# Attention and routed experts on one core: remainders of 64 rows as transposes, two PTb buffers, spread weight loads

## The chip, the cores and the metric

The kernel runs on one core of one Trainium2 chip. The metric is the time of one execution on the device in microseconds (us), the median of several runs. A second number comes from a profiled execution: its span, from the first to the last instruction. Engines: PE is TensorE's matmul queue, PEld its weight loads, DVE the vector engine, ACT the scalar engine, POOL is GpSimd, SP issues most DMAs.

## The reference

Eight batches of eight heads, 576 positions, head size 64. Attention keeps only the scores within `tau` of a row's maximum; its output becomes the input of a mixture of experts with one chosen expert of eight for each token.

```python
scores = scale * q @ k.T
thresh = max(scores, axis=-1) - tau
scores = where(scores >= thresh, scores, -1e9)
attn = exp(scores - max(scores)); attn = attn / (sum(attn) + 1e-9)
x = (attn @ v), heads side by side              # 4608 tokens x 512
e = argmax(x @ w_gate)                          # one expert of 8
y = relu(x @ w1[e]) @ w2[e]                     # 512 -> 1024 -> 512
out = softmax(x @ w_gate)[e] * sigmoid(x @ w_output_gate)[e] * y
```

## The kernel before, in words

There are two stages: attention (to about 480 us), then the experts. All engines but SP run in the order in which the program writes their instructions, so the order of the Python code is the order of each engine's queue.

A unit is one head of two batches, side by side as the two halves `a` = 0, 1 of 64 partitions. There are 32 units, two to an iteration `m`, and 16 iterations of `T` = 9 steps (`run`, L319). The step is `s`, the running number `g`. A step takes one block `t` of 128 query rows: steps 0 to 3 the blocks of the even unit, 5 to 8 those of the odd one, and step 4 the last 64 rows of both.

In step `g` the following is issued:

- `scores` (L129): PE computes scores into `ps` (two buffers of two banks for a step); DVE copies them out scaled, with the row minimum (L152); POOL makes the threshold `thr` (L159).
- In steps 1 and 5 `x_rows` (L283): PE turns the finished X of an earlier unit into rows and router logits, in the two single banks `pr` (pool `ps_r`) and `pa` (pool `ps_a`). ACT copies them out as `xl` (L345). The first write goes to `pr`.
- `exps` (L162): two exponentials on ACT, `p` from `s`, one for each half.
- V products by the table `AV` (`av_units`, L236): ten products of transposed probabilities with V for one unit, spread over steps 6, 7, 8, 0 (even unit) and 2, 3, 4 (odd). Four go into `pa`; a middle one takes the remainder rows for both banks and ends with the copy of X out of `pa` (L251); four go into `pb`, a tile of the bank `pr`, and end with the copy of X out of it (L258), in steps 0 and 4. The middle one is in steps 2 and 7, which are `CROSS`.
- The transposes of step `g - 2`: keys lie in 9 pieces of 128, of which the ninth holds the 64 remaining keys of both halves. `blocks` (L220) turns the first eight pieces by 16 transposes of 64 rows (L226) into `pt` (two banks, one buffer), which ACT copies to PTa or PTb (L231, L234). `remainder` (L199) turns the ninth.
- The masks of step `g - 1` on DVE (L179), which read `p`.
- `logits`, `inverse` (L267: an addition and a reciprocal on DVE, 128x10), hooks, and a step of the router (`rt.advance`).

`remainder` has two forms. In steps 1, 3, 5, 6 and 8 it is two transposes of 64 rows (L203), each into a corner of a bank that is open at that time or fresh, with one ACT copy each (L208). In steps 0, 2, 4 and 7 it is a pair of full products with the identity (L211; each is two instructions in the trace) into one bank, and one ACT copy (L216). In steps 2 and 7 they are issued ahead of the middle V product, into the bank that `pb` will use.

PTa holds the transposed probabilities of query rows 0 to 255, PTb those of the other 320, each in one buffer. The last 64 rows of the odd unit are produced before PTb is free for that unit, so they go to PTc, and a DMA on ACT's queue (L382) moves them to PTb in step 0.

Experts: a raw weight chunk is two loads of 512 KB (`load`, L793); four raw buffers. The hook at `end - 15` steps (L1238) calls `begin`, which issues four chunks, each after the latest `thr` (the gate). POOL scatters finished rows by indirect DMA (L531) in the meantime.

Of the kernel before, what the change touches and what calls it, by code (L numbers as in the profile page):

```python
# [20 lines left out]
class Attention:  # L21
# [6 lines left out]
    AV = {0: (-2, 2), 2: (-1, 4), 3: (-1, 2), 4: (-1, 2), 6: (0, 3), 7: (0, 1), 8: (0, 2)}  # L28
    CROSS = (2, 7)
    ROWS = {1: -2, 5: -1}  # L30
    LOGITS = {3: -2, 7: -1}
    INVERSE = ((7, 0), (2, 1))
# [70 lines left out]
    def warm_up(self, n):  # L103
        nc = self.nc
        wt = self.w2.tile([P, 512], BF16, name="wt")
        nc.vector.memset(wt, 0.0)
        self.wt = wt
        self.keep_warm(n)
# [79 lines left out]
    def turned(self, u, t):  # L188
        if t == 0:
            self.PTa = self.w2.tile([P, self.NK, self.QA], F32, name="PTa")  # L190
        if t == 2:
            self.PTb = self.w2.tile([P, self.NK, self.S - self.QA], F32, name="PTb")
        if t == self.NB:
            self.PTc = self.w2.tile([P, self.NK, 64], F32, name="PTc")
            return [self.PTb[:, :, self.QA :], self.PTc]
        q = self.PTa if t < 2 else self.PTb
        return [q[:, :, t % 2 * P : t % 2 * P + P]]

    def remainder(self, dst, p, pair=None, fresh=2, rest=None):  # L199
        nc, hs, M, RB = self.nc, self.half, self.M, self.NK - 1  # L200
        if pair:
            for h in range(2):
                nc.tensor.matmul(  # L203
                    pair[h], p[hs[h], M : M + P], self.ident[hs[h], hs[h]], start=h == fresh or fresh > 1, stop=True,
                    is_transpose=True, skip_group_check=True,
                )
            at = lambda h: dst[0][:, RB, 64 * h : 64 * h + 64] if len(dst) == 1 else dst[h][:, RB]
            return lambda h: nc.scalar.copy(at(h), pair[h])  # L208
        for pp in hs:
            o = M + pp.start  # L210
            nc.tensor.matmul(rest[pp, 0:P], p[:, o : o + 64], self.ident, start=True, stop=True, skip_group_check=True)  # L211

        def out():
            w = P // len(dst)
            for h, d in enumerate(dst):
                nc.scalar.copy(d[:, RB], rest[:, h * w : h * w + w])  # L216

        return out

    def blocks(self, dst, p, outs=()):  # L220
        nc, id_, hs, RB = self.nc, self.ident, self.half, self.NK - 1
        pt = self.ps_t.tile([P, 1024], F32, name="pt")
        for b in range(RB):
            for h in range(2):
                o, k0 = h * 512 + b * 64, (b + b // 4) * P
                nc.tensor.transpose(pt[:, o : o + 64], p[hs[h], k0 : k0 + P], id_[hs[h], hs[h]])  # L226
        for f in outs:
            f()
        if len(dst) == 1:
            d = dst[0][:, 0:RB].rearrange("p b (h j) -> p b h j", j=64)  # L230
            nc.scalar.copy(d, pt.rearrange("p (h b j) -> p b h j", h=2, j=64))  # L231
        else:
            for h, d in enumerate(dst):
                nc.scalar.copy(d[:, 0:RB], pt[:, h * 512 : h * 512 + 512].rearrange("p (b j) -> p b j", j=64))  # L234

    def av_units(self, u):  # L236
# [10 lines left out]
        pb, N = self.bank(), self.PTb.shape[2]  # L247
# [14 lines left out]
    def bank(self):  # L262
        if self.pb is None:
            self.pb = self.ps_r.tile([P, 512], F32, name="pr")
        return self.pb

    def inverse(self, m, i):  # L267
        if i == 0:
            self.rinv[m] = self.w3.tile([P, 2, 10], F32, name="rinv", bufs=2)
        r, s = self.rinv[m][:, i], self.sums[m][:, i]  # L270
        self.nc.vector.tensor_scalar(r, s, 1e-9, None, op0=ALU.add)
        self.nc.vector.reciprocal(r, r)
        if i:
            self.sums.pop(m)
# [44 lines left out]
    def run(self, hooks):  # L319
        nc, T, G, rt = self.nc, self.T, self.G, self.router  # L320
        W, NB = self.XW, self.NB
        st, pr, av, xls, later, held = {}, {}, {}, {}, None, None
        self.prep_first()
        for g in range(G + self.TAIL):
# [12 lines left out]
            if xu is not None:  # L337
# [3 lines left out]
                if turn:  # L341
                    out = self.remainder(dst, pr[g2], [x[:, 5 * W : 5 * W + 64] for x in ps])
                xl = xls[xu] = self.w2.tile([P, 2, 5, W], F32, name="xl")
                for a in (1, 0):
                    nc.scalar.copy(xl[:, a].rearrange("p j w -> p (j w)"), ps[a][:, 0 : 5 * W])  # L345
                    if turn:
                        out(a)
# [8 lines left out]
            if turn and xu is not None:  # L356
                self.blocks(dst, pr.pop(g2))
            soon = s in self.EARLY or g == G - 1
            if g < G and not soon:
                pr[g] = self.exps(u, t, *st[g])  # L360
            if s in self.AV:
                du, n = self.AV[s]
                au = 2 * m + du
                if 0 <= au < self.nu:
# [4 lines left out]
                    if s in self.CROSS:  # L369
                        if turn:  # L370
                            dst, o = [], self.S - self.QA
                            held = self.remainder(dst, pr[g2], rest=self.bank()[:, o : o + P])
                        next(av[au])
            if turn and xu is None:
                p = pr.pop(g2)
                u2, t2 = self.at(g2)
                if held is None:
                    dst = []
                dst.extend(self.turned(u2, t2))
                if u2 % 2 and t2 == 2:  # L380
                    if g < G:
                        nc.scalar.dma_start(self.PTb[:, :, self.QA :], self.PTc)  # L382
                pair = None
                if self.pa is not None:
                    rest = self.ps_r.tile([P, 512], F32, name="pr")
                    pair = [self.pa[:, self.S - self.QA : self.S - self.QA + 64], rest[:, 0:64]], 1
                elif self.pb is not None and held is None:
                    rest = self.ps_a.tile([P, 512], F32, name="pa")
                    pair = [rest[:, 0:64], self.pb[:, 448:512]], 0
                if pair:  # L390
                    out = self.remainder(dst, p, *pair)
                    outs = [lambda: out(0), lambda: out(1)]
                elif held:
                    outs = [held]
                else:
                    rest = self.ps_a.tile([P, 512], F32, name="pa")
                    outs = [self.remainder(dst, p, rest=rest)]
                if soon:
                    for f in outs:
                        f()  # L400
                    outs = []
                    if g < G:
                        pr[g] = self.exps(u, t, *st[g])
                self.blocks(dst, p, outs)
                held = None
# [3 lines left out]
            if g == G:  # L409
                nc.vector.tensor_copy(self.PTb[:, :, self.QA :], self.PTc)  # L410
# [6 lines left out]
            for at, i in self.INVERSE:  # L417
                if s == at and 0 <= m - i < self.nu // 2:
                    self.inverse(m - i, i)
# [341 lines left out]
class Experts:  # L761
# [101 lines left out]
    def begin(self):  # L863
# [7 lines left out]
        self.halves, self.ready = [], []  # L871
# [7 lines left out]
    def load_next(self):  # L879
        while self.nload < min(len(self.seq), self.nsplit + self.RB):  # L880
# [341 lines left out]
def build(tc, qkv, tau, wg, w1, w2, out, shape):  # L1222
    nc = tc.nc
    with ExitStack() as ctx:
# [6 lines left out]
        with tc.manual_schedule(engines=ENGINES):  # L1231
            with ExitStack() as actx:
# [5 lines left out]
                hooks[end - 3 * T] = lambda: ex.begin()  # L1238
# [71 lines left out]
```

## Time and profile before

| what | us |
|---|---|
| median of 3 runs | 932.99 |
| lowest and highest run | 931.55, 935.29 |
| the profiled execution: its time | 935.04 |
| the profiled execution: its span | 933.3 |
| PE busy, DVE busy, ACT busy | 922.0, 695.6, 597.2 |

The span is 1.7 us shorter than the time of the same execution; what lies around it belongs to no instruction. Busy time of PE is an upper bound of its work, since its instructions overlap and their ends are modelled; the start times are what to go by. A PEld shown as idle for 0.4 us between two groups of different tile shape is mostly that change of shape.

### The profile page before, as it was taken

Reading aid. Unit: us, or ns where it says so; the run is one execution under the profiler, and the core shown is the slowest. Engines: PE = TensorE matmul, PEld = TensorE weight load, DVE = VectorE, ACT = ScalarE, POOL = GpSimd, SP = SyncE. Lnnn points to the kernel's source line nnn. Section 1 sums busy time; section 2 is a strip of 40 time slices with the busy share of each in tenths; the row PEclk is TensorE's granted clock in tenths of the full one; section 3 lists DMA queues with packets and bytes.
Section 4 is the critical chain, followed back from the end, with each engine's and each line's share of the span. In section 5 each row is a group of like instructions: output and inputs, shape, how many; then the busy total and the mean of one; then the engine's idle time right before and its main releaser. Section 6 shows DMA issues by size and latency. Waiting matters only on the chain.

```text
span 933.3 us, 22373 instructions
## 1 busy us (share of the span) xinstructions
PE 922.0 (99%) x8477; PEld 699.1 (75%) x8477; DVE 695.6 (75%) x1749; ACT 597.2 (64%) x1105; POOL 381.9 (41%) x641
## 2 busy tenths in 40 slices
PE   9999999999999999999999999999999999999997
PEld 5666676666666766665778888878988888988885
DVE  6999999999999999999876876646446436456631
ACT  6898888989889898887863543335335335345521
POOL 4455655768757785566746610202102101103001
PEclk9999999999999999999999999999999999999999
DMA  5386432233422432327237882427536436536301
GB/s 167 116 262 230 146 96 64 88 92 108 137 81 70 134 118 85 93 58 257 72 124 230 272 277 91 152 95 243 180 136 196 157 123 213 175 120 224 128 19 45
DMA packets 87661, 132.36 MB, mean 142 GB/s; under 512 B 23953, under 2 KB 50833, under 8 KB 87552
## 3 DMA queue, kind: packets, MB, share of 16 engines
q1 hardware_dynamic: 63488, 106.07, 35.5%
q0 software_dynamic: 6544, 20.42, 5.9%
q10 hardware_dynamic: 17520, 4.42, 2.1%
q8 instruction: 67, 1.10, 0.5%
q14 instruction: 42, 0.34, 0.1%
HBM read 95.26 MB, written 32.20 MB: 137 GB/s over the span
## 4 chain that ended last, share of the span: by engine, by line
PE 93%; DVE 2%; ACT 2%; issue 2%; DMA 1%; POOL 1%; DVEq 0%; POOLq 0%; ACTq 0%
PE ps L141 16%; PE pr L242 8%; PE pt L226 8%; PE pa L242 8%; PE ph L1017 8%; PE ph L1018 7%; PE ph L1019 7%; PE py L1040 5%; PE py L1038 5%; PE py L1039 5%; PE pr L289 3%; PE py L1133 2%; PE py L1134 2%; PE py L1132 2%; PE pa L289 1%
## 5 line engine op out<-in xcount | busy, mean ns | idle before, releaser
L166 ACT ACTIVATE p<-s,mn 128x576 f32<-128x576 f32 x288 | 209.8, 794 | 40.8 <-DVE s L152 37.3
L179 DVE SCALAR_TENSOR_TENSOR p<-s,thr,p 128x576 f32<-128x576 f32 x288 | 224.4, 816 | 1.9 <-POOL thr L159 1.9
L152 DVE TENSOR_SCALAR_CACHE_REDUCE s<-ps 128x576 f32<-128x576 f32 x288 | 205.5, 750 | 25.0 <-PE ps L141 22.2
L141 PE MATMUL ps<-qk 64*128 64x288 f32 (+1 forms) x1280 | 183.6, 420 | 0.1
L838 POOL DMA_INDIRECT out_dram<-yo,kid x39 | 45.6, 1169 | 333.5 <-DVE yo L837 257.4
L159 POOL TENSOR_SCALAR thr<-mn,tau_sb 128x2 f32<-128x2 f32 x144 | 105.7, 734 | 151.4 <-DVE s L152 149.0
L1021 ACT ACTIVATE hh<-ph 128x256 fp32r<-128x256 f32 (+3 forms) x103 | 49.7, 482 | 181.9 <-PE ph L1019 171.2
L1017 PE MATMUL ph<-xh,w1h 128*128 128x256 f32 (+3 forms) x412 | 139.5, 339 | 0.0
L1018 PE MATMUL ph<-xl,w1h 128*128 128x256 f32 (+3 forms) x412 | 136.6, 332 | 0.2 <-DVE xl L850 0.2
L1019 PE MATMUL ph<-xh,w1l 128*128 128x256 f32 (+3 forms) x412 | 136.4, 331 | 0.0
L1022 DVE SCALAR_TENSOR_TENSOR hl<-ph,hh 128x256 fp32r<-128x256 f32 (+3 forms) x103 | 55.5, 539 | 101.7 <-ACT hh L1021 100.9
L141 PEld LDWEIGHTS ps<-qk 64*128 64x128 f32 (+1 forms) x1280 | 108.6, 178 | 18.4 <-DVE s L152 3.0
L242 PE MATMUL pr<-PTb,vld 128*64 128x320 f32 (+1 forms) x640 | 108.3, 451 | 0.2 <-DMA PTb<-PTc 0.2
L226 PEld LDWEIGHTS pt<-ident,p 64*128 64x128 f32 x2304 | 84.6, 138 | 22.2 <-ACT p L166 7.4
L226 PE MATMUL pt<-ident,p 64*128 64x64 f32 x2304 | 100.2, 225 | 0.6 <-ACT PTa L231 0.6
L242 PE MATMUL pa<-PTa,vld 128*64 128x256 f32 (+1 forms) x640 | 87.4, 391 | 0.1
L1040 PE MATMUL py<-w2h,hl 128*128 128x512 f32 x213 | 84.3, 396 | 0.9 <-DVE hl L1022 0.9
L850 DVE TENSOR_TENSOR w1l<-r,w1h 128x1024 fp32r<-128x1024 f32 x52 | 63.6, 1223 | 28.0 <-ACT w1h L847 24.9
L1038 PE MATMUL py<-w2h,hh 128*128 128x512 f32 x213 | 84.2, 395 | 0.0
L1017 PEld LDWEIGHTS ph<-xh,w1h 128*128 128x128 f32 x412 | 77.4, 188 | 8.9
L1039 PE MATMUL py<-w2l,hh 128*128 128x512 f32 x213 | 84.0, 394 | 0.0
L1018 PEld LDWEIGHTS ph<-xl,w1h 128*128 128x128 f32 x412 | 77.4, 188 | 7.8 <-DVE xl L850 0.6
(217 smaller groups left out, 1643.5 us busy)
## 6 DMA issues: line engine op xcount, KB each, us to landing
r<-in_moe_w_dram SPq DMA_DIRECT2D x104, 512.0 KB
qk<-in_qkv_dram SPq DMA_DIRECT2D x31, 608.0 KB
xs<-zrow SPq DMA_DIRECT2D x41, 257.0 KB
vld<-in_qkv_dram SPq DMA_DIRECT2D x32, 320.0 KB
PTb<-PTc ACTq DMA_DIRECT2D x15, 288.0 KB
xg<-xs SPq DMA_DIRECT2D x4, 771.0 KB
xg<-xs SPq DMA_DIRECT2D x6, 514.0 KB
xg<-xs SPq DMA_DIRECT2D x3, 1028.0 KB
```

What stands on the lines that cost most here:

```text
L141: nc.tensor.matmul(ps[a][rows, o : o + HS], q[pp, t * P : t * P + w], k[pp, k0 : k0 + HS], start=True, stop=True)
L152: nc.vector.tensor_scalar(s, ps[a][:, c0 : c0 + S], SC, None, op0=ALU.mult, op1=ALU.min, accum_out=mn[:, a : a + 1])
L166: self.nc.scalar.activation(e, s, AF.Exp, bias=mn[:, a : a + 1], scale=-1.0)
L179: nc.vector.scalar_tensor_tensor(e, s, thr[:, a : a + 1], e, op0=ALU.is_le, op1=ALU.mult, accum_out=acc[:, a ^ (t > 1) : (a ^ (t > 1)) + 1])
L226: nc.tensor.transpose(pt[:, o : o + 64], p[hs[h], k0 : k0 + P], id_[hs[h], hs[h]])
L242: one = lambda out, l, r, start, stop: nc.tensor.matmul(out, l, r, start=start, stop=stop, skip_group_check=True)
L1017: nc.tensor.matmul(ph, w1h[:, c, fs], self.xh[:, c, 0:N], start=(c == 0), stop=False)
L1018: nc.tensor.matmul(ph, w1h[:, c, fs], self.xl[:, c, 0:N], start=False, stop=False)
L1019: nc.tensor.matmul(ph, w1l[:, c, fs], self.xh[:, c, 0:N], start=False, stop=(c == 3))
L1038: nc.tensor.matmul(Y, hh[:, ts], wh, start=(f == 0), stop=False)
L1039: nc.tensor.matmul(Y, hh[:, ts], wl, start=False, stop=False)
L1040: nc.tensor.matmul(Y, hl[:, ts], wh, start=False, stop=(f == 7))
```

## The change

- Steps 0, 2, 4 and 7 get the transposes of 64 rows too. `spots` says where each half goes. With both banks free (steps 0 and 4): half 0 into a fresh `pa` ahead of the sixteen transposes, half 1 into a fresh `pr` behind them. In steps 2 and 7: half 1 into columns 320 to 383 of the open `pb` ahead of them, half 0 into a fresh `pa` behind them. The copies of those ahead are issued on ACT ahead of those behind.
- `LATE`: in steps 0, 4 and 7 the exponentials are issued behind the V products and their copy of X, and ahead of the remainder's copies.
- PTb has two buffers; the odd unit's one is made early and takes the rows that went to PTc. The DMA from PTc, and the DVE copy of it at the end, go.
- The inverse's addition goes to GpSimd, one step ahead of the reciprocal, which stays on DVE.
- Four weight chunks are issued at `end - 30`, `- 24`, `- 18` and `- 12` instead of all at `end - 15`.
- In the step after the last scores the transposes use a bank pair of `ps`. The zeros for PE's warm-up lie in X[1].

```diff
...
     LB = 3
     VB = 4
     WARM = {0: 4, 1: 2}
-    AV = {0: (-2, 2), 2: (-1, 4), 3: (-1, 2), 4: (-1, 2), 6: (0, 3), 7: (0, 1), 8: (0, 2)}
+    AV = {0: (-2, 2), 2: (-1, 5), 3: (-1, 2), 4: (-1, 2), 6: (0, 3), 7: (0, 2), 8: (0, 2)}
     CROSS = (2, 7)
+    LATE = (0, 4, 7)
     ROWS = {1: -2, 5: -1}
     LOGITS = {3: -2, 7: -1}
-    INVERSE = ((7, 0), (2, 1))
+    INVERSE = ((6, 0, 0), (7, 0, 1), (1, 1, 0), (2, 1, 1))
     ROUTE = (0, 2, 4, 6, 8)
     TAIL = 6
     EARLY = (6,)
...
     def turned(self, u, t):
         if t == 0:
             self.PTa = self.w2.tile([P, self.NK, self.QA], F32, name="PTa")
+        wide = lambda: self.w2.tile([P, self.NK, self.S - self.QA], F32, name="PTb", bufs=2)
         if t == 2:
-            self.PTb = self.w2.tile([P, self.NK, self.S - self.QA], F32, name="PTb")
+            self.PTb = self.odd if u % 2 else wide()
         if t == self.NB:
-            self.PTc = self.w2.tile([P, self.NK, 64], F32, name="PTc")
-            return [self.PTb[:, :, self.QA :], self.PTc]
+            self.odd = wide()
+            return [x[:, :, self.QA :] for x in (self.PTb, self.odd)]
         q = self.PTa if t < 2 else self.PTb
         return [q[:, :, t % 2 * P : t % 2 * P + P]]
-    def remainder(self, dst, p, pair=None, fresh=2, rest=None):
-        nc, hs, M, RB = self.nc, self.half, self.M, self.NK - 1
-        if pair:
-            for h in range(2):
-                nc.tensor.matmul(
-                    pair[h], p[hs[h], M : M + P], self.ident[hs[h], hs[h]], start=h == fresh or fresh > 1, stop=True,
-                    is_transpose=True, skip_group_check=True,
-                )
-            at = lambda h: dst[0][:, RB, 64 * h : 64 * h + 64] if len(dst) == 1 else dst[h][:, RB]
-            return lambda h: nc.scalar.copy(at(h), pair[h])
-        for pp in hs:
-            o = M + pp.start
-            nc.tensor.matmul(rest[pp, 0:P], p[:, o : o + 64], self.ident, start=True, stop=True, skip_group_check=True)
-
-        def out():
-            w = P // len(dst)
-            for h, d in enumerate(dst):
-                nc.scalar.copy(d[:, RB], rest[:, h * w : h * w + w])
-
-        return out
-
-    def blocks(self, dst, p, outs=()):
+    def remainder(self, p, h, to, start=True):
+        hs, M = self.half[h], self.M
+        self.nc.tensor.matmul(
+            to, p[hs, M : M + P], self.ident[hs, hs], start=start, stop=True, is_transpose=True, skip_group_check=True
+        )
+
+    def rest_out(self, dst, h, src):
+        RB = self.NK - 1
+        self.nc.scalar.copy(dst[0][:, RB, 64 * h : 64 * h + 64] if len(dst) == 1 else dst[h][:, RB], src)
+
+    def spots(self, crossed):
+        a, b = self.S - self.QA, 448
+        fresh = lambda pool, name: pool.tile([P, 512], F32, name=name)[:, 0:64]
+        A, B = (self.ps_a, "pa"), (self.ps_r, "pr")
+        if self.pa is not None:
+            return [(0, self.pa[:, a : a + 64], False), (1, fresh(*B), True)], ()
+        if self.pb is None:
+            return [(0, fresh(*A), True)], [(1, fresh(*B), True)]
+        if crossed:
+            return [(1, self.pb[:, a : a + 64], False)], [(0, fresh(*A), True)]
+        return [(0, fresh(*A), True), (1, self.pb[:, b : b + 64], False)], ()
+
+    def blocks(self, dst, p, spots=(), spare=False):
         nc, id_, hs, RB = self.nc, self.ident, self.half, self.NK - 1
-        pt = self.ps_t.tile([P, 1024], F32, name="pt")
+        pool, name = (self.ps_s, "ps") if spare else (self.ps_t, "pt")
+        pt = pool.tile([P, 1024], F32, name=name)
         for b in range(RB):
             for h in range(2):
                 o, k0 = h * 512 + b * 64, (b + b // 4) * P
                 nc.tensor.transpose(pt[:, o : o + 64], p[hs[h], k0 : k0 + P], id_[hs[h], hs[h]])
-        for f in outs:
-            f()
+        for h, to, start in spots:
+            self.remainder(p, h, to, start)
+            self.rest_out(dst, h, to)
         if len(dst) == 1:
             d = dst[0][:, 0:RB].rearrange("p b (h j) -> p b h j", j=64)
             nc.scalar.copy(d, pt.rearrange("p (h b j) -> p b h j", h=2, j=64))
...
             for a in range(2):
                 one(pa[hs[a], 0:Q], vm[:, kb, a], self.PTa[:, 4 * a + kb], kb == 0, False)
             yield
-        pb, N = self.bank(), self.PTb.shape[2]
+        pb, N = self.ps_r.tile([P, 512], F32, name="pr"), self.PTb.shape[2]
+        self.pb = pb
         for a in range(2):
             one(pa[hs[a], 0:Q], vm[hs[a], self.NB, a], self.PTa[hs[a], RB], False, True)
             one(pb[hs[1 - a], 0:N], vm[hs[a], self.NB, a], self.PTb[hs[a], RB], True, False)
...
                 self.pb = None
             yield
-    def bank(self):
-        if self.pb is None:
-            self.pb = self.ps_r.tile([P, 512], F32, name="pr")
-        return self.pb
-
-    def inverse(self, m, i):
-        if i == 0:
-            self.rinv[m] = self.w3.tile([P, 2, 10], F32, name="rinv", bufs=2)
-        r, s = self.rinv[m][:, i], self.sums[m][:, i]
-        self.nc.vector.tensor_scalar(r, s, 1e-9, None, op0=ALU.add)
-        self.nc.vector.reciprocal(r, r)
-        if i:
-            self.sums.pop(m)
+    def inverse(self, m, i, last):
+        if not last:
+            if i == 0:
+                self.rinv[m] = self.w3.tile([P, 2, 10], F32, name="rinv", bufs=2)
+            r = self.rinv[m][:, i]
+            self.nc.gpsimd.tensor_scalar(r, self.sums[m][:, i], 1e-9, None, op0=ALU.add)
+            if i:
+                self.sums.pop(m)
+        else:
+            r = self.rinv[m][:, i]
+            self.nc.vector.reciprocal(r, r)
     def rows(self, bp):
         rt = self.router
...
     def run(self, hooks):
         nc, T, G, rt = self.nc, self.T, self.G, self.router
         W, NB = self.XW, self.NB
-        st, pr, av, xls, later, held = {}, {}, {}, {}, None, None
+        st, pr, av, xls, later = {}, {}, {}, {}, None
         self.prep_first()
         for g in range(G + self.TAIL):
             m, s = divmod(g, T)
...
                 ps = self.x_rows(xu)
                 if turn:
                     dst = self.turned(*self.at(g2))
-                if turn:
-                    out = self.remainder(dst, pr[g2], [x[:, 5 * W : 5 * W + 64] for x in ps])
+                rest = [x[:, 5 * W : 5 * W + 64] for x in ps]
+                for h in range(2) if turn else ():
+                    self.remainder(pr[g2], h, rest[h])
                 xl = xls[xu] = self.w2.tile([P, 2, 5, W], F32, name="xl")
                 for a in (1, 0):
                     nc.scalar.copy(xl[:, a].rearrange("p j w -> p (j w)"), ps[a][:, 0 : 5 * W])
                     if turn:
-                        out(a)
+                        self.rest_out(dst, a, rest[a])
                 self.x_out(xu, xl, 0)
                 if g < G:
                     later = xu, xl
...
                 later = None
             if turn and xu is not None:
                 self.blocks(dst, pr.pop(g2))
+            run = lambda: pr.update({g: self.exps(u, t, *st[g])}) if g < G else None
             soon = s in self.EARLY or g == G - 1
-            if g < G and not soon:
-                pr[g] = self.exps(u, t, *st[g])
+            if not soon and s not in self.LATE:
+                run()
             if s in self.AV:
                 du, n = self.AV[s]
                 au = 2 * m + du
...
                         av[au] = self.av_units(au)
                     for _ in range(n):
                         next(av[au])
-                    if s in self.CROSS:
-                        if turn:
-                            dst, o = [], self.S - self.QA
-                            held = self.remainder(dst, pr[g2], rest=self.bank()[:, o : o + P])
-                        next(av[au])
+            if not soon and s in self.LATE:
+                run()
             if turn and xu is None:
                 p = pr.pop(g2)
-                u2, t2 = self.at(g2)
-                if held is None:
-                    dst = []
-                dst.extend(self.turned(u2, t2))
-                if u2 % 2 and t2 == 2:
-                    if g < G:
-                        nc.scalar.dma_start(self.PTb[:, :, self.QA :], self.PTc)
-                pair = None
-                if self.pa is not None:
-                    rest = self.ps_r.tile([P, 512], F32, name="pr")
-                    pair = [self.pa[:, self.S - self.QA : self.S - self.QA + 64], rest[:, 0:64]], 1
-                elif self.pb is not None and held is None:
-                    rest = self.ps_a.tile([P, 512], F32, name="pa")
-                    pair = [rest[:, 0:64], self.pb[:, 448:512]], 0
-                if pair:
-                    out = self.remainder(dst, p, *pair)
-                    outs = [lambda: out(0), lambda: out(1)]
-                elif held:
-                    outs = [held]
-                else:
-                    rest = self.ps_a.tile([P, 512], F32, name="pa")
-                    outs = [self.remainder(dst, p, rest=rest)]
+                dst = self.turned(*self.at(g2))
+                first, last = self.spots(s in self.CROSS)
+                for h, to, start in first:
+                    self.remainder(p, h, to, start)
+                for h, to, _ in first:
+                    self.rest_out(dst, h, to)
                 if soon:
-                    for f in outs:
-                        f()
-                    outs = []
-                    if g < G:
-                        pr[g] = self.exps(u, t, *st[g])
-                self.blocks(dst, p, outs)
-                held = None
+                    run()
+                self.blocks(dst, p, last, g == G)
             g1 = g - 1
             if 0 <= g1 < G:
                 self.masks(*self.at(g1), *st.pop(g1), pr[g1])
-            if g == G:
-                nc.vector.tensor_copy(self.PTb[:, :, self.QA :], self.PTc)
             lu = 2 * m + self.LOGITS[s] if m and s in self.LOGITS else None
             if g >= G:
                 lu = xu
             if lu is not None and lu in xls:
                 self.logits(lu, xls.pop(lu), nc.gpsimd if g < G else nc.vector)
             late = m >= self.nu // 2 - 6
-            for at, i in self.INVERSE:
+            for at, i, last in self.INVERSE:
                 if s == at and 0 <= m - i < self.nu // 2:
-                    self.inverse(m - i, i)
+                    self.inverse(m - i, i, last)
             if g in hooks:
                 hooks[g]()
             rt.advance(s in self.ROUTE or late, s not in self.ROWS or g >= G)
...
         self.make, self.units = make, {}
         self.seq = [(i, g) for i in range(len(make)) for g in range(4)]
         self.nload = self.done = self.used = self.nsplit = 0
-        self.halves, self.ready = [], []
+        self.halves, self.ready, self.ahead = [], [], 0
+
+    def more(self):
+        self.ahead += 1
         self.load_next()
     def unit(self, i):
...
         return self.units[i]
     def load_next(self):
-        while self.nload < min(len(self.seq), self.nsplit + self.RB):
+        while self.nload < min(len(self.seq), self.nsplit + self.ahead):
             i, g = self.seq[self.nload]
             if not self.known(i):
                 return
...
                 hooks = {2 * T: lambda: rt.queue.append(rt.init_units())}
                 end = at.G
                 ws = []
-                hooks[end - 3 * T] = lambda: ex.begin()
+                hooks[end - 31] = lambda: ex.begin()
+                for i in range(ex.RB):
+                    hooks[end - 30 + 6 * i] = ex.more
                 hooks[end - 1] = lambda: (ws.extend(ex.first_chunk()), ex.unit(0).gather())
                 hooks[end + 1] = lambda: (ws[0](), ws[1]())
```

## Rows read from the trace of the kernel before

**Rows 1.** The page's first part: busy us (share of the span) and instructions of each engine.

```profile
PE 922.0 (99%) x8477; PEld 699.1 (75%) x8477; DVE 695.6 (75%) x1749; ACT 597.2 (64%) x1105; POOL 381.9 (41%) x641
```

**Rows 2.** Windows: stretch, length, busy PE, PEld, DVE, ACT, POOL; clock, DMA share, GB/s.

```profile
210.22:238.81 28.59, 28.59 (x379) 19.34 (x375) 27.09 (x79) 25.70 (x51) 22.96 (x31) 1.00 0.43 138
383.27:413.94 30.67, 30.67 (x382) 20.37 (x378) 30.37 (x93) 26.23 (x53) 20.18 (x40) 1.00 0.25 72
413.94:446.31 32.37, 31.23 (x377) 20.14 (x374) 27.98 (x80) 25.82 (x51) 21.14 (x32) 0.95 0.61 205
438.00:441.00 3.00, 2.91 (x15) 1.27 (x13) 3.00 (x9) 2.58 (x5) 2.68 (x5) 0.77 0.56 217
```

**Rows 3.** Timeline of PE, steps 0 to 3: start, us, engine, line, what, xcount.

```profile
349.73 1.30 PE L242 MATMUL pr<-PTb,vld 128*64 128x320 f32 x8
...
351.73 1.19 PE L141 MATMUL ps<-qk 64*128 64x288 f32 x8
352.75 0.23 PE L289 MATMUL pr<-wx,X 64*128 64x80 f32 x1
...
358.95 1.20 PE L141 MATMUL ps<-qk 64*128 64x288 f32 x8
```

**Rows 4.** Timeline of PE, steps 7 and 8.

```profile
344.09 0.39 PE L211 MATMUL pr<-ident,p 128*64 128x128 f32 x4
344.41 0.43 PE L242 MATMUL pa<-PTa,vld 64*64 64x256 f32 x1
...
344.74 0.44 PE L242 MATMUL pr<-PTb,vld 64*64 64x320 f32 x2
...
346.77 1.30 PE L242 MATMUL pr<-PTb,vld 128*64 128x320 f32 x8
...
348.12 0.66 PE L226 MATMUL pt<-ident,p 64*128 64x64 f32 x16
348.61 1.19 PE L141 MATMUL ps<-qk 64*128 64x288 f32 x8
```

**Rows 5.** Timeline of PE at the end of attention.

```profile
471.45 0.71 PE L226 MATMUL pt<-ident,p 64*128 64x64 f32 x16 [0.64 <-ACT PTa L231]
...
477.59 2.38 PE L242 MATMUL pr<-PTb,vld 128*64 128x320 f32 x16
```

**Rows 6.** Timeline of ACT at the end of attention.

```profile
470.39 1.01 ACT L231 COPY PTa<-pt 128x1024 f32<-128x1024 f32 x1
...
480.01 0.43 ACT L258 COPY X<-pr 128x320 f32<-128x320 f32 x1 [1.07 <-PE pr L242]
```

**Rows 7.** Timeline of ACT, steps 8 to 2 of the quiet iteration.

```profile
349.04 0.19 ACT L208 COPY PTa<-pa 128x64 f32<-128x64 f32 x1
349.13 0.21 ACT L208 COPY PTa<-pr 128x64 f32<-128x64 f32 x1
...
350.64 1.46 ACT L166 ACTIVATE p<-s,mn 128x576 f32<-128x576 f32 x2 [0.21 <-DVE s L152]
...
352.00 0.41 ACT L258 COPY X<-pr 128x320 f32<-128x320 f32 x1
352.31 0.27 ACT L216 COPY PTb<-pa 128x128 f32<-128x128 f32 x1
...
358.70 0.39 ACT L251 COPY X<-pa 128x256 f32<-128x256 f32 x1
```

**Rows 8.** Waits in 20 to 470 us: who for whom, us, times, longest.

```profile
PEld pr L242 <- ACT PTa L208: 11.8, 28, 0.8
...
POOL sums L186 <- DMA xs<-rows,dsti: 4.6, 2, 4.4
...
PEld pr L242 <- DMA PTb<-PTc: 0.6, 1, 0.6
```

**Rows 9.** Two lines by source: count, duration in ns (min/median/max), first and last start.

```profile
L159 POOL TENSOR_SCALAR thr<-mn,tau_sb x144: 289/789/824, 8.1 to 468.9; 128x2 f32<-128x2 f32 x144
...
L271 DVE TENSOR_SCALAR rinv<-sums x32: 161/426/577, 28.9 to 477.6; 128x10 f32<-128x10 f32 x32
```

More of the change, by code (lines that the diff above doesn't have):

```diff
@@ L104, in warm_up @@
         nc = self.nc
-        wt = self.w2.tile([P, 512], BF16, name="wt")
+        wt = self.X[1][:, 0:256]
         nc.vector.memset(wt, 0.0)
-        self.wt = wt
+        self.wt = wt.bitcast(BF16)
         self.keep_warm(n)
```

## The prediction

> **What bounds the kernel now.** I read the page first: TensorE (PE) is busy for 922.0 of 933.3 us, the vector engine (DVE) for 695.6 and the scalar engine (ACT) for 597.2 [rows 1]. Shares of the whole span hide stages, so next came the windows, one for each iteration (two units, nine steps). A quiet iteration takes 28.59 us; in it PE has no gap, but DVE is busy for 27.09 and ACT for 25.70 [rows 2]. PE sets the pace, and the other two have only 1.5 and 2.9 us to spare. So the thing to ask of this change is not only what PE no longer does, but for whom PE now waits. Two iterations are longer: one of 30.67 us, in which DVE is busy for 30.37, so that DVE sets it, and one of 32.37 us [rows 2]. Then I laid PE's timeline beside that of ACT for a quiet iteration. In step 0 the products with the values (V products) start at 349.73 and end 1.30 later, the next scores start at 351.73, and `x_rows` of step 1 at 352.75, that is 1.02 after those scores: PE waits for nothing [rows 3].
>
> **PE work removed.** From the start of the V products to the next scores it takes 2.00 us in step 0, with the full products, and 1.84 in step 8 (346.77 to 348.61), which already has the two transposes [rows 3, 4]. So steps 0 and 4 can give 0.16 each. In step 7 the four L211 instructions hold PE from 344.09 to 344.41. About 0.11 of that I count as the gap at the change of tile shape, which stays: four V products that end in the L211 shape are followed without one. Two more transposes come back for about 0.06, twice the spacing of the sixteen (348.12 to 348.61) [rows 4]. That leaves 0.15 in step 7, and in step 2, which has the same order. All four together: 0.62 us in an iteration, if nothing waits.
>
> **The waits that come in.** A bank goes to its next user when the last copy out of it has ended. In steps 0 and 4 ACT's new order is: the copy of X, two exponentials, then the copies of the two 64-row remainders, the second of them out of the bank that `x_rows` writes first.
>
> Steps 0 and 4, then 1 and 5: the V products end at 349.73 + 1.30 = 351.03 [rows 3]. ACT starts 0.04 after a modelled end of PE where it waits for one (477.59 + 2.38, then 480.01) [rows 5, 6]. So the copy of X starts at 351.07. Its slot is 0.31 (352.00 to 352.31), two exponentials take 1.36 (350.64 to 352.00), the first remainder copy 0.09, and the second ends 0.21 after its start (349.04, 349.13): 351.07 + 0.31 + 1.36 + 0.09 + 0.21 = 353.04 [rows 7]. PE follows a copy by 0.05 (470.39 + 1.01, then 471.45) [rows 5, 6], so `x_rows` starts at 353.09 instead of 352.75: 0.34 late, although the scores ahead of it come 0.1 earlier. The exponentials' own input is no limit: before, both ran from 350.64 on without a gap. Behind `x_rows` in PE's queue stand the transposes and the next scores, so it goes straight into the pace. Steps 4 and 5 have the same order: 0.68 together.
>
> Step 2: the remainder of half 0 now goes into the bank that the copy of X out of `pa` frees, and on ACT that copy stands behind the exponentials of two steps. It starts at 358.70, right behind them, and ends at 359.09; PE can follow at 359.14 and start the scores about 0.08 later, at 359.22 and not 358.95 [rows 7, 3]. Both chains begin at the end of `x_rows`, so this is 0.27 on top. Without the wait PE would be there at 358.80.
>
> Steps 7 and 8: the products end at 344.74 + 0.44 - 0.21 = 344.97, the copy of X (256 columns; 0.25, from the 0.31 for 320) starts at 345.01, the exponentials take 1.36, and the copy of the remainder, now out of the open bank `pb`, ends 0.21 later, at 346.83. The V products of step 8 write that bank. Freed of the full products they could start at 346.62 instead of 346.77; if they must wait for this copy, it is 346.88, 0.11 late [rows 4, 7]. That they wait I take from the waits: products into `pr` are released by copies `PTa<-pr` 28 times [rows 8], and the products read nothing of what these copies write. (Most of the 0.4 us each is the change of tile shape; what counts is that the order is kept.) The Trainium skill, "PSUM — Partial Sum Buffer", section "PSUM bank collisions raise a hardware error", says it more sharply: guard by bank and quadrant, not by address, for two engines in one bank are an error even at disjoint columns. It speaks against parking a remainder in an open bank; guarded by address alone, the sum would be 0.26 x 16 = 4 us less.
>
> Sum of an iteration: 0.34 + 0.34 + 0.27 + 0.11 = 1.06 us longer; 15 iterations have all four: +15.9 us. Bounds: every wait hidden, -0.62 x 15 = -9.3; each wait 0.1 longer, +22.
>
> **What else it moves.** Weight loads: in the iteration of 32.37 us (DMA share 0.61) eight loads are issued one behind the other on SP; GpSimd (POOL) then waits 4.4 us at L186, and the granted clock is 0.77 over the 3 us after PE's gap, a mean of its levels 2.4 and 1.2 GHz [rows 2, 8]. That iteration costs 32.37 - 28.59 = 3.8 us. In the change SP issues two loads at a time, six steps apart, each behind the thr of its step as before; behind them on SP stands at most the load of q and k for two units later, ten steps ahead of its use. I take 3.2, bounds 0 and 3.8. The DMA from `PTc` held PE once, for 0.6 [rows 8]: -0.6, bounds 0 and 0.6. Its issue on ACT's queue lies beneath the exponentials, and the second PTb buffer ends no other wait that I find. In the step after the last scores PE idles 0.64 for its bank [rows 5]; the spare one gives 0.6, bounds 0 and 0.9. In the iteration that DVE sets, 2.1 us over a quiet one, a later PE costs less: -1.5 with a little of others, bounds 0 and 2.5.
>
> The inverse's addition: 32 of some 0.43 us leave DVE and cost POOL at most 0.82 each, the longest of another small operation there [rows 9]. I cost it at nothing: DVE has 1.5 us an iteration to spare, POOL is busy for 22.96 of 28.59 [rows 2], and the reciprocal comes a step later. If it held DVE up and that spare time were gone, 32 x 0.82 = 26 us; if DVE set the pace, it would give 14. The later exponentials cost nothing of their own: the masks that read them come a step later.
>
> Sum: 935.04 + 15.9 - 3.2 - 0.6 - 0.6 - 1.5 = 945.0 us for the profiled execution. That one lies 2.05 above the median of 932.99, so the forecast is 943 us, 1.1% slower. Half a per cent, 4.7 us, is about what a measurement of this kernel tells from no change.
>
> **The rivals.**
> A, faster: the waits stay hidden. Place: `x_rows` in steps 1 and 5. It is decided by whether the second remainder copy ends by 352.70. Price: -9.3 - 3.2 - 0.6 - 0.6, so 919 us. For it: ends on PE are modelled, and PE has most of the work removed. Against: two exponentials of 0.68 stand on ACT between the end of the V products and that copy, and only 1.72 us lie between that end and `x_rows`. Chance 0.17.
> B, no change: only the waits ahead of `x_rows` hold, those of steps 2 and 8 don't: (0.68 - 0.30) x 15 = +5.7, less 5.9: 933 us. For it: step 2's wait is the difference of two long chains. Against: ACT shows no gap ahead of that copy. Chance 0.16.
> C, the spread loads hold POOL at L186 all the same: 3.2 more, 946 us. For it: two are still 1 MB at once. Chance 0.05.
> D, the clock: if each of the 60 new waits were followed by 3 us at 0.77, each would lose 0.7: +42, 985 us. Against: quiet iterations, with 144 transposes each, are granted 1.00 [rows 2]. The Trainium skill, "TensorE: Matmul & The Clock Gate", section "Part 4: PE-mode transpose", holds that transposes don't count as busy for the clock the way matmuls do; by that a kernel with more of them is nearer to the fall. Chance 0.03.
> The forecast, 0.59, has its own range of 937 to 949, each wait being uncertain by about 0.1 (15 x 4 x 0.1 = 6).
>
> **How the numbers follow.** 926 to 951 holds the forecast's range, B, C and the upper edge of A: about 0.8. Slower by over 0.5% (above 937.7): 0.57 of the forecast, C, D and a little of B, 0.67. Within it: most of B, 0.17. Faster: nearly all of A, 0.16.
>
> **What would show it.** Right: `x_rows` starts about 1.4 us after its scores, released by an ACT copy; a PE gap of 0.4 ahead of the last remainder in step 2; quiet iterations of about 29.6 us; no L186 wait of 4 us and no iteration of 32. Wrong: quiet iterations of 28.0 us with `x_rows` 1.02 after its scores; or V products of step 8 that start while the copy out of `pb` still runs.

## The result, and the profile after

| kernel | median us | ratio to the kernel before, 95% interval |
|---|---|---|
| before | 932.99 | |
| changed | 947.36 (four of the five runs: 945.67 to 948.00) | 1.0149 [1.0134, 1.0163] |
| changed, second series | 946.65 | 1.0140 [1.0119, 1.0160] |

The change makes the kernel 1.4 to 1.5% slower; 943 us (937 to 949) and the direction were forecast. The fifth run, a profiled one, had a granted clock of 0.85 from start to end and took 1003.76 us, for a reason that stays open, so the ratio leaves it out and the rows below are of an execution in the second series, with a granted clock of 0.998 and a span of 945.8 us.

First the windows of this kernel: a quiet iteration, counted from step 0, and the one with the last weight loads.

```profile
329.72:359.52 29.80, 28.93 (x368) 18.62 (x366) 26.61 (x75) 25.75 (x55) 22.45 (x34) 1.00 0.38 128
...
419.57:449.82 30.25, 29.37 (x368) 18.91 (x366) 27.62 (x80) 26.43 (x56) 19.85 (x34) 1.00 0.45 147
```

The quiet iteration grew from 28.59 [rows 2] to 29.80 us, and PE, which had no gap, now has 0.87 us of them. DVE is busy for less than before (26.61 for 27.09) and ACT for as long (25.75 for 25.70). The timeline of PE shows where, from step 8 to the start of step 3:

```profile
356.40 1.24 PE L142 MATMUL ps<-qk 64*128 64x288 f32 x8
357.69 1.30 PE L247 MATMUL pr<-PTb,vld 128*64 128x320 f32 x8
...
360.65 1.30 PE L247 MATMUL pr<-PTb,vld 128*64 128x320 f32 x8
...
362.49 1.29 PE L142 MATMUL ps<-qk 64*128 64x288 f32 x8
364.03 0.33 PE L293 MATMUL pr<-wx,X 64*128 64x80 f32 x1 [0.25 <-ACT PTb L209]
364.20 0.27 PE L293 MATMUL pr<-wx,X 64*128 64x80 f32 x1
...
369.46 0.77 PE L230 MATMUL pt<-ident,p 64*128 64x64 f32 x16
370.55 0.27 PE L203 MATMUL pa<-ident,p 64*128 64x64 f32 x1 [0.32 <-ACT X L257]
370.56 1.29 PE L142 MATMUL ps<-qk 64*128 64x288 f32 x8
```

And the timeline of ACT beside it:

```profile
357.44 0.20 ACT L209 COPY PTa<-pr 128x64 f32<-128x64 f32 x1
...
362.00 0.43 ACT L264 COPY X<-pr 128x320 f32<-128x320 f32 x1 [0.86 <-PE pr L247]
362.32 1.44 ACT L167 ACTIVATE p<-s,mn 128x576 f32<-128x576 f32 x2
363.66 0.20 ACT L209 COPY PTb<-pa 128x64 f32<-128x64 f32 x1
363.75 0.22 ACT L209 COPY PTb<-pr 128x64 f32<-128x64 f32 x1
...
370.11 0.39 ACT L257 COPY X<-pa 128x256 f32<-128x256 f32 x1
```

Read them together. `x_rows` (L293) starts 1.54 after its scores, where it was 1.02 [rows 3]: it waits for the second remainder copy, which ends at 363.75 + 0.22 = 363.97. That copy stands behind two exponentials, and these behind the copy of X, for which ACT idles 0.86. In step 2 the last remainder comes 1.09 after the first of the sixteen transposes (0.55 of it is their own time), released by the copy of X that ends at 370.50. In step 8 the V products start 1.29 after their scores, 0.05 after the copy `PTa<-pr` has ended. Before it was 1.12: the V products of step 8 at 346.77 [rows 4], behind these scores:

```profile
345.65 1.19 PE L141 MATMUL ps<-qk 64*128 64x288 f32 x8
```

The waits of the whole stretch say it in sums (who for whom, us, times, longest):

```profile
ACT X L264 <- PE pr L247: 26.1, 30, 0.9
PEld pr L293 <- ACT PTb L209: 20.5, 29, 0.7
...
PE pr L293 <- ACT PTb L209: 7.4, 29, 0.3
PE pa L203 <- ACT X L257: 4.7, 15, 0.3
```

The second and third row are one event each time: weight loads and products of `x_rows` waiting, 29 times, twice an iteration. In the trace such a wait is a semaphore of the program, which ACT's copies raise.

### The profile page after: what moved, and what is told of

It reads as the page before. It is cut to its first block, busy times and chain, and to the rows that moved or that the text cites. A ratio compares the mean times of both kernels' runs of the same rounds, so it can differ in the third digit from the quotient of the medians.

```text
span 1002.0 us, 22227 instructions
## 1 busy us (share of the span) xinstructions
PE 988.2 (99%) x8345; PEld 705.8 (70%) x8345; DVE 687.3 (69%) x1716; ACT 602.0 (60%) x1171; POOL 376.2 (38%) x673
## 5 line engine op out<-in xcount | busy, mean ns | idle before, releaser
L142 PE MATMUL ps<-qk 64*128 64x288 f32 (+1 forms) x1280 | 198.8, 457 | 0.0
L1000 PE MATMUL ph<-xh,w1h 128*128 128x256 f32 (+3 forms) x412 | 145.7, 354 | 0.0
L1001 PE MATMUL ph<-xl,w1h 128*128 128x256 f32 (+3 forms) x412 | 142.7, 346 | 0.2 <-DVE xl L830 0.2
L1002 PE MATMUL ph<-xh,w1l 128*128 128x256 f32 (+3 forms) x412 | 142.7, 346 | 0.0
L142 PEld LDWEIGHTS ps<-qk 64*128 64x128 f32 (+1 forms) x1280 | 112.4, 185 | 16.9 <-DVE s L153 2.0
L247 PE MATMUL pr<-PTb,vld 128*64 128x320 f32 (+1 forms) x640 | 118.2, 483 | 0.3
L247 PE MATMUL pa<-PTa,vld 128*64 128x256 f32 (+1 forms) x640 | 94.9, 431 | 0.3 <-ACT PTb L209 0.3
L1022 PE MATMUL py<-w2l,hh 128*128 128x512 f32 x213 | 88.8, 417 | 0.0
L1023 PE MATMUL py<-w2h,hl 128*128 128x512 f32 x213 | 88.7, 417 | 0.0
L1021 PE MATMUL py<-w2h,hh 128*128 128x512 f32 x213 | 88.5, 416 | 0.0
L1002 PEld LDWEIGHTS ph<-xh,w1l 128*128 128x128 f32 x412 | 79.8, 194 | 8.0
```

The source lines that it names most:

```text
L142: nc.tensor.matmul(ps[a][rows, o : o + HS], q[pp, t * P : t * P + w], k[pp, k0 : k0 + HS], start=True, stop=True)
L247: one = lambda out, l, r, start, stop: nc.tensor.matmul(out, l, r, start=start, stop=stop, skip_group_check=True)
L1000: nc.tensor.matmul(ph, w1h[:, c, fs], self.xh[:, c, 0:N], start=(c == 0), stop=False)
L1001: nc.tensor.matmul(ph, w1h[:, c, fs], self.xl[:, c, 0:N], start=False, stop=False)
L1002: nc.tensor.matmul(ph, w1l[:, c, fs], self.xh[:, c, 0:N], start=False, stop=(c == 3))
L1022: nc.tensor.matmul(Y, hh[:, ts], wl, start=False, stop=False)
```

## The experiments

Ten kernels ran, in three series; each ratio is to the kernel before in the same series.

**The changed kernel once more.** No edit.

> The changed kernel once more, for its times and a trace at full clock. Theory (copies out of a bank hold PE): about 947 us; in a quiet iteration x_rows of steps 1 and 5 starts 1.35 to 1.5 us after its scores and not 1.02, the last remainder of step 2 comes 0.4 us after its last transpose, the V products of step 8 start 1.25 us or more after their scores and not 1.12, and the iteration is about 29.6 us. Rival (no such waits; the loss is in the loads, the router or the end of attention): x_rows 1.02 after its scores, quiet iterations of 28.0 us, and the 14 us stand in a few long iterations.

946.65 us and the rows above: 1.54, a last remainder 0.54 late, 1.29, and 29.80 us. All four waits are there (`x_rows` has two an iteration), and the loss is spread over the quiet iterations. The rival is out.

**Steps 0 and 4: copies ahead of the exponentials.** To the changed kernel:

```diff
+    LAST = (0, 4)
...
-            if not soon and s in self.LATE:
+            last_of_all = turn and not soon and s in self.LAST
+            if not soon and s in self.LATE and not last_of_all:
                 run()
...
                 self.blocks(dst, p, last, g == G)
+                if last_of_all:
+                    run()
```

> Steps 0 and 4 only: the exponentials go behind the remainder's copies and the copy of the transposes. Theory: x_rows of steps 1 and 5 starts 1.02 after its scores again; that ends two waits of 0.34 and lets the 0.16 of each of these steps through, up to 1.0 us in each of 15 iterations, 932 us; up to 0.2 each may come back since the copies of x_rows on ACT then stand behind later exponentials, 937 us. Rival (the waits ahead of x_rows are not these copies): 947 us, within 2.

934.97 us, ratio to before 1.0026 [1.0013, 1.0038]: 11.7 us of the loss gone by the order of two steps. PE's timeline, then ACT's:

```profile
354.46 1.29 PE L143 MATMUL ps<-qk 64*128 64x288 f32 x8
355.53 0.23 PE L294 MATMUL pr<-wx,X 64*128 64x80 f32 x1
```

```profile
354.76 0.21 ACT L210 COPY PTb<-pr 128x64 f32<-128x64 f32 x1 [0.25 <-PE pr L204]
354.87 1.02 ACT L237 COPY PTb<-pt 128x1024 f32<-128x1024 f32 x1
355.78 1.45 ACT L168 ACTIVATE p<-s,mn 128x576 f32<-128x576 f32 x2
357.12 0.49 ACT L351 COPY xl<-pa 128x400 f32<-128x400 f32 x1
```

`x_rows` is back at 1.07 after its scores. The quiet iteration is 28.93, not the 28.8 of a full cure: the copy of `xl` starts only when the later exponentials let it, and step 2, which hangs on that chain, takes 4.97 and not 4.80. That is about the 0.2 that the expectation left open.

**Step 2 late too.** `LATE = (0, 2, 4, 7)` in the changed kernel.

> Step 2 only: its exponentials go behind the V products and their copy of X too. Theory: the bank of the last remainder of step 2 comes free 0.4 us earlier, the gap ahead of it closes, 0.27 + 0.15 = 0.42 us in each of 15 iterations: 941 us. Rival (the wait in step 2 is the difference of two long chains and not there): no gap before it either, 947 us; if the later exponentials hold up the masks, slower than 947.

940.14 us, 1.0077 [1.0060, 1.0094]: 6.5 us gained. PE's timeline:

```profile
364.55 0.77 PE L230 MATMUL pt<-ident,p 64*128 64x64 f32 x16
365.10 0.26 PE L203 MATMUL pa<-ident,p 64*128 64x64 f32 x1
```

The last remainder now follows the sixteen at once, 0.55 after their start where it was 1.09. The wait in step 2 was real and was that copy of X. The quiet iteration is 29.47, so 0.34 of the 0.42 came through: step 3 is 0.15 longer than in the changed kernel, by a wait that the run of all three orders shows below.

**Step 7: the open bank's copy ahead of the exponentials.**

```diff
+    FIRST = (7,)
...
-            if not soon and s in self.LATE:
+            after_first = turn and not soon and s in self.FIRST
+            if not soon and s in self.LATE and not after_first:
                 run()
...
-                if soon:
+                if soon or after_first:
                     run()
```

> Step 7 only: the copy of the remainder out of the open bank goes ahead of the exponentials. Theory (products and copies exclude each other by bank): the V products of step 8 start 1.12 after their scores, 0.26 us in each of 16 iterations is won: 943 us. Rival (excluded by columns only): they never waited, 947 us.

944.33 us, 1.0120 [1.0100, 1.0141]: 2.3 us gained, about half of what was expected, and no overlap of the kind the rival needs. PE's timeline, then ACT's:

```profile
354.47 1.24 PE L143 MATMUL ps<-qk 64*128 64x288 f32 x8
355.64 1.30 PE L248 MATMUL pr<-PTb,vld 128*64 128x320 f32 x8
```

```profile
354.16 0.22 ACT L210 COPY PTa<-pr 128x64 f32<-128x64 f32 x1
354.26 1.45 ACT L168 ACTIVATE p<-s,mn 128x576 f32<-128x576 f32 x2
```

With the copy early, the V products start 1.17 after their scores and not 1.29. So a product into columns 0 to 319 of `pb` did wait for a copy out of columns 320 to 383. The wait was 0.12, not 0.26, because the scores of step 8 themselves came later than I had them: the sixteen transposes of step 7 wait for the bank pair `pt`. They start 0.06 after the last copy out of it has ended, at 352.75 + 1.11 = 353.86:

```profile
352.75 1.11 ACT L240 COPY PTb<-pt 128x512 f32<-128x512 f32 x2
353.92 0.71 PE L231 MATMUL pt<-ident,p 64*128 64x64 f32 x16
```

**All three orders.** The three edits together.

> The three reorderings of the runs before together: step 2 late too, in step 7 the open bank's copy ahead of the exponentials, in steps 0 and 4 all copies ahead of them. Theory (each wait is its own, on PE's path): the three gains add up, 946.7 - 11.7 - 6.5 - 2.3 = 926 us, quiet iterations of 28.3 to 28.5 us. Rival (the waits share one cause, ACT's backlog, so that one order cures most of it, or DVE now sets the pace): 930 to 934 us.

930.81 us, 0.9957 [0.9939, 0.9974]: the sum of the three was 926. Quiet iterations are 28.47, as the theory had it, and there the gains do add up: alone they were 0.88, 0.34 and 0.12, together 29.81 - 28.47 = 1.34. The time ended where the rival had it. Five longer iterations (28.99 to 29.74 now) won only 0.5 to 0.8 each, which makes 3.5 us less over iterations 1 to 14; what sets their length was not tried. One more wait was visible, in step 3 (PE, then ACT):

```profile
328.75 1.22 PE L144 MATMUL ps<-qk 64*128 64x288 f32 x8
330.11 1.30 PE L249 MATMUL pr<-PTb,vld 128*64 128x320 f32 x8
```

```profile
329.86 0.20 ACT L211 COPY PTa<-pr 128x64 f32<-128x64 f32 x1
```

1.36 from scores to V products: with step 2 late, its own copy out of the open `pb` now stands behind its exponentials. It is the wait of step 8 over again.

**Four orders.** `FIRST = (2, 7)` on top.

> The three reorderings together, and in step 2 the copy out of the open bank ahead of the exponentials as well. In the run of three, the V products of step 3 started 1.36 after their scores and not 1.12, released by that copy. Theory: this wait goes, 0.24 us in each of 15 iterations, 3.6 us: 927 us. Rival (something else holds step 3, or DVE sets the pace now): 931 us.

926.09 us, 0.9926 [0.9911, 0.9941]. This version beats both kernels, by 0.7% and 2.1%. Of the 4.7 us under the run of three, 0.20 stand in each quiet iteration, 3 us in all; the rest is within that run's own range of 927.58 to 932.32. PE's timeline and the window of a quiet iteration:

```profile
326.09 1.23 PE L144 MATMUL ps<-qk 64*128 64x288 f32 x8
327.24 1.30 PE L249 MATMUL pr<-PTb,vld 128*64 128x320 f32 x8
```

```profile
316.02:344.28 28.26, 28.26 (x370) 19.15 (x366) 26.38 (x75) 25.74 (x56) 22.02 (x33) 1.00 0.40 128
```

1.15, near the 1.12 of before, and PE without a gap.

**The spread loads alone**, in the kernel before: the hooks at `end - 31` and `end - 30 + 6 * i`.

> The kernel before with the spread weight loads alone. Theory (eight loads at once starve POOL at L186): no wait of 4 us there, the iteration of 32.4 us is under 29.5, 3.2 us gained: 930 us. Rival (two loads of 512 KB hold POOL as well, or the wait is the scatter's own): 933 us.

931.44 us, 0.9968 [0.9950, 0.9985], against 933.94 for the kernel before in the same series: 2.5 us gained. L186 no longer appears among its waits.

**Two PTb buffers alone**, in the kernel before.

> The kernel before with two PTb buffers alone: no PTc, no DMA on ACT's queue. Theory: only the one wait of 0.6 to 0.8 us for that DMA goes, 932.4 us. Rival (the DMA's issue holds up ACT in each iteration): 0.3 us or more in each of 15, 928 us or less.

932.30 us, 0.9984 [0.9967, 1.0001]: 1.6 us, just within the uncertainty. Quiet iterations are unchanged at 28.57 to 28.60, so the rival, a cost in each of them, is out. The wait that the theory removes is not in every execution: the run with the loads alone still has that DMA and shows no wait for it.

**The inverse's addition alone**, in the kernel before.

> The kernel before with the inverse's addition on GpSimd alone. Theory: DVE is behind PE, so 32 additions off it give nothing but a little in the iteration that DVE sets: 932 to 933 us. Rivals: DVE is the pace after all, 0.4 in each step that had one, 920 us; or the reciprocal now waits for GpSimd, 936 us or more.

932.79 us, 0.9991 [0.9974, 1.0008]: no difference that can be told. Quiet iterations stay at 28.57 to 28.59. These two kernels still have the old loads, and each shows the wait at L186 (first the one with two PTb buffers):

```profile
POOL sums L186 <- DMA xs<-rows,dsti: 3.4, 1, 3.4
```

```profile
POOL sums L186 <- DMA xs<-rows,dsti: 3.0, 1, 3.0
```

**All of the change but the remainder**, in the kernel before: loads, PTb, the inverse and the spare bank.

> The kernel before with everything of the change except the remainder and its order: spread loads, two PTb buffers, the inverse's addition on GpSimd, the spare bank at the end. Theory: these gains stand beside each other, 2.5 + 1.6 + 0.6 or less + 1.1 or less: 929 us; then the new remainder in its own order is what costs some 18 us, and in the best order it is worth 2 us. Rival (they gain nothing together): 933 us.

929.30 us, 0.9962 [0.9947, 0.9976], 4.0 us under its series' 933.25. The changed kernel stands some 17 us above it: that is the new remainder in its own order. The best order, which ran in the same series, is 3.2 us below it.

## Why the prediction was right, point by point

**PE work removed.** Steps 0 and 4 give what was said: scores to scores 2.97 and 2.96, from 3.12 each. Not all of the 0.62 came through: even with four orders mended the quiet iteration is 28.27, 0.32 under the kernel before. Steps 0, 2 and 4 then give 0.15 to 0.17 each, but step 7 only 0.02 of its 0.15, since its transposes wait for `pt`, and steps 1, 3, 5 and 8 are 0.04 to 0.05 longer each.

**The waits.** The chain for steps 0 and 1, added up from rows of ACT, put `x_rows` 353.09 - 349.73 = 3.36 after the start of the V products; it measured 364.03 - 360.65 = 3.38. Lengths of steps, from the starts of their scores in quiet iterations:

| steps | before | changed | longer by | forecast |
|---|---|---|---|---|
| 0, 1 | 5.77 | 6.24 | 0.47 | 0.34 |
| 2, 3 | 7.63 | 7.95 | 0.32 | 0.27 |
| 4, 5, 6 | 9.06 | 9.41 | 0.35 | 0.34 |
| 7, 8 | 6.12 | 6.21 | 0.09 | 0.11 |
| iteration | 28.6 | 29.8 | 1.2 | 1.06 |

The mechanism was right at all four places, and three runs show it by taking it away: steps 0 and 4 together, step 2, step 7. The sum was too small by 0.15. The start time of `x_rows` was right to 0.02, but after the stop its second product came 0.17 behind the first, where it was 0.07 in the kernel before; this restart was not in the sum.

Two rows of the table agree in part by luck. Steps 4 and 5 alone grew by 0.46, as steps 0 and 1 did, and step 6 gave 0.11 back that nobody had forecast: its V products start 1.13 after their scores where it was 1.24. In steps 7 and 8 the forecast saved 0.15 and then waited 0.26; measured were 0.07 and 0.17.

**By bank, not by column.** The Trainium skill, "PSUM — Partial Sum Buffer", section "PSUM bank collisions raise a hardware error", asks for a guard by bank and quadrant. The trace agrees with that: products started 0.05 after a copy from other columns of their bank, and the run with that copy moved ahead gained 2.3 us. It shows that this program keeps such a guard, by a semaphore; what happens without one no run here shows.

**The rest.** Loads: 2.5 measured for 3.2 forecast; the sizing came from one execution, in which L186 waited 4.4 us, and the two other executions with old loads show 3.4 and 3.0. The iteration of 32.37 us [rows 2] takes 29.82 now, as any quiet one.

The spare bank was put at 0.6, and the trace shows nothing of it. The wait of 0.64 ahead of the transposes [rows 5] is gone, but two others stand right behind them: the last remainder waits for the copy of X, and `x_rows` for the remainder's copy:

```profile
480.97 0.77 PE L230 MATMUL ps<-ident,p 64*128 64x64 f32 x16
482.29 0.27 PE L203 MATMUL pr<-ident,p 64*128 64x64 f32 x1 [0.56 <-ACT X L264]
482.86 0.33 PE L293 MATMUL pr<-wx,X 64*128 64x80 f32 x1 [0.30 <-ACT PTb L209]
```

From the start of the last scores to that of the last V product it is 13.93 us in the changed kernel and 13.35 before. With all but the remainder it is 13.37, so the spare bank won nothing there either. That all side parts together measured 4.0 for 4.4 forecast is thus partly luck.

What the iteration set by DVE gives back was put at 1.5, "with a little of others". The scores of iteration 1 start at 31.28 in the changed kernel and 30.97 before, those of iteration 15 at 449.82 and 438.19: 11.3 us longer over 14 iterations. 14 x 1.21 = 16.9 would be the waits alone. Of the 5.6 between them, 1.4 is the stop at L186, as far as it lies in this stretch, and 0.8 the one wait for the DMA from PTc. That leaves 3.4, more than the upper bound of 2.5: the iteration of 30.67 [rows 2] takes 30.68 now and so gives back 1.2, and four others, of 28.73 to 29.59 before, grew by 0.4 to 1.1 instead of 1.21 and give back 2.0 together. That DVE sets the first of these is not shown: it is busy for 29.36 us of it now and for 30.37 before, and the length is the same. The addition on GpSimd took 0.25 in the median, far under the bound of 0.82:

```profile
L273 POOL TENSOR_SCALAR rinv<-sums x32: 250/251/613, 25.6 to 489.0; 128x10 f32<-128x10 f32 x32
```

**The rivals.** A and B fall with the first experiment, C with the spread loads alone. D does too: with some 60 waits the windows above were granted 1.00. The Trainium skill, "TensorE: Matmul & The Clock Gate", section "Part 4: PE-mode transpose", holds that transposes don't count as busy for the clock the way matmuls do. The trace shows no fall from it: an iteration of 162 transposes among its products keeps the upper level, 2.4 GHz.

In sum the forecast was 4 us low. Its terms beside what the two profiled executions show (933.3 and 945.8 us of span), worked out from the starts of scores (the waits are 16.9 and 1.1 for the last iteration, the loads 1.4 and 2.3 in the step behind, where the granted clock fell):

| term | forecast | measured |
|---|---|---|
| the waits | +15.9 | +18.0 |
| weight loads | -3.2 | -3.7 (-2.5 by medians) |
| DMA from PTc | -0.6 | -0.8 |
| end of attention, spare bank | -0.6 | +0.6 |
| longer iterations | -1.5 | -3.4 |
| start and experts' stage | 0 | +1.9 |
| sum | +10.0 | +12.5 |

The direction and the waits follow from the working. That the sum came as near as 4 us owes something to errors that cancel: the waits and the end of attention cost 3.3 more than forecast, and the longer iterations gave back 1.9 more. The last term is mostly in the first quarter of the experts' products, which took 110.8 to 112.8 us in eleven profiled executions, whatever the kernel.

## What to carry to other kernels

When a bank is handed on, time not the instruction that fills it but the last copy out of it, and look at what stands ahead of that copy on its engine. Here a hoped-for saving of 0.6 us an iteration became a loss of 1.2, most of it because two exponentials were issued between the end of the products and two copies of 0.2 us each; moving the same instructions turned 947 us into 926. In this program a result parked in a corner of an open bank also makes the bank's next product wait for its copy.

## What was not expected of the hardware

At `x_rows` PE paid for a stop twice. When it had waited, its first product took 0.33 instead of 0.23 and the second came 0.17 later instead of 0.07, so a stop cost about 0.1 us more than its wait. In the runs that ended this wait the second product came 0.07 later again.

GpSimd was held for 3.0 to 4.4 us at a copy of 64 elements, with a scatter DMA named as the releaser, in three executions with eight weight loads of 512 KB issued at once. With two at a time the same copy waited 1.2 us at most, in eight executions, and not at all in the run with the loads alone. Why this copy waits for a scatter was not tried.
